# Reordering a decode-attention pipeline: earlier and deeper K/V loads, and an output projection with the weights held still

## The chip, the cores and the metric

The kernel runs on one core of one Trainium2 chip. The metric is the device time of one execution in microseconds, read several times. The span in a profile is about 1.8 us shorter than the time of the same run. "The Trainium skill" is a set of notes on the chip; where the text leans on one of its pages, it names the page.

The engines go by their names in the profile: PE multiplies matrices (its stationary operand, the "weights", is loaded first and the other streams past it), DVE is the vector engine, ACT the scalar engine, POOL is GpSimd, and SyncE (SP) issues the loads. PSUM is the memory that the matmuls add into. The granted clock is PE's clock in the records, as a share of full speed. A hole is a stretch in which the DMA engines are not full; the tail is the time from the last landing of a load to the end.

## The reference

Two independent decode-attention problems, A and B, each for 4 sequences with one new token. There are 32 query heads, 8 K/V heads (4 query heads share one), a window of the last 2048 cache rows and head size 128.

```python
W = min(4096, max(256, Sk // 4))                 # 2048
q = (x @ wq).reshape(B, 1, 32, 128)              # x [4,1,512], wq [512,4096]
k = k_cache[:, :, Sk - W:, :]                    # [4, 8, 2048, 128], likewise v
p = softmax(q k^T * 128**-0.5)
o = p v
y = o.reshape(B, 1, 4096) @ wo                   # wo [4096,512]
return concatenate([y_A, y_B], axis=-1)          # [4,1,1024], bfloat16
```

One (sequence, K/V head) pair is called a chunk: 0.5 MB of K and 0.5 MB of V. There are 64 chunks. With the weights (4 MB of wq and 4 MB of wo for each problem) the kernel reads 84 MB and does little arithmetic on it.

## The kernel before

Chunks run in groups of eight: two K/V heads ("halves") of four sequences. For each chunk K is loaded, DVE transposes it, and four matmuls add its scores to one PSUM bank that holds the whole group. After the eighth chunk come row maximum, exponential, a transpose of the probabilities and the row sums. Then each chunk's V is multiplied (16 small matmuls, "PV"), DVE normalises, and the output projection runs. All loads are issued by SyncE, in program order, so a wait in that list holds back everything behind it:

```python
NK, NKB, NV, BT_LEAD = 4, 4, 4, 2     # raw K, transposed K, V buffers; transposes ahead
PV_OFF = GC + 1                       # GC = 8; PV runs 9 steps after the scores
KV = PV_OFF + 1                       # K loads run 10 steps ahead of V loads

def issue_k(c):
    if c >= NK:
        sp.wait_ge(s_bt, c - NK + 1)      # transposes of K done
    sp.dma_start(kraw[:, c % NK, :], k_src(c)).then_inc(...)
def issue_v(c):
    if c >= NV:
        sp.wait_ge(s_pv, c - NV + 1)      # PV done
    sp.dma_start(vraw[:, c % NV, :], v_src(c)).then_inc(...)

issue_k(0); ...x loads, wq pieces of problem A...
for c in range(1, min(KV, NTOT)):
    issue_k(c)                            # ...and pieces of wo
for s in range(NTOT):
    if s + KV < NTOT:
        issue_k(s + KV)
    issue_v(s)
    ...                                   # pieces of wo and of problem B's wq
```

The projection streams 512 columns of weights past a stationary of 4 columns. The weights are loaded with one head dimension per partition, so every row in DRAM is 512 bfloat16 numbers, 1 KB:

```python
def wo_src(P):
    return probs[P][4].rearrange("(h d) c -> d h c", d=128)
...
for h in range(rep):                                     # do_oproj, per half
    pe.matmul(pob[0:Bsz, 0:D], oT_sb[:, P, hg, :], wo_sb[:, P, hg, :], ...)
```

## Time and profile before

| | before |
|---|---|
| time, median of 3 runs | 230.9 us |
| span of the profiled run | 230.0 us |
| busy: PE / DVE | 146.4 / 102.4 us |
| moved by DMA | 84.16 MB, mean 366 GB/s |

The profiled run (231.78 us) was labelled "slow" in the records. It lies inside the range of later runs of this kernel labelled fast (up to 232.88 us), and a variant of this kernel profiled in a fast run (b1_earlyv below) has nearly the same loss at the end, so I use its structure, not differences of a tenth.

These are the two DMA rows of the page's 40 slices (5.75 us each): busy share of the 16 DMA engines in tenths, and GB/s.

```profile
DMA  6998889999999999999999999999999999999640
GB/s 192 420 416 303 251 269 407 401 399 413 415 415 406 417 392 391 409 396 394 403 392 351 411 393 407 388 402 392 409 385 397 410 395 393 407 392 353 268 180 1
```

There are two holes: slices 4 to 6 (303, 251, 269) and the last four. The windows view puts numbers on them. Its columns are the stretch in us, its length, busy us and instruction count of PE, weight loads, DVE, ACT and POOL, then the granted clock, the DMA share and GB/s.

```profile
0.00:6.00 6.00, 0.00 (x0) 0.00 (x0) 1.25 (x1) 1.28 (x1) 4.83 (x18) 1.00 0.68 198
6.00:20.00 14.00, 3.75 (x131) 3.70 (x132) 1.93 (x3) 0.00 (x0) 5.31 (x1) 1.00 1.01 414
20.00:34.00 14.00, 10.13 (x38) 3.80 (x36) 10.13 (x10) 0.60 (x1) 6.32 (x24) 0.96 0.83 248
34.00:210.00 176.00, 121.06 (x1331) 61.03 (x1338) 86.30 (x105) 7.31 (x17) 11.14 (x40) 0.70 1.03 399
210.00:224.00 14.00, 7.94 (x140) 4.95 (x138) 2.04 (x5) 0.08 (x1) 0.00 (x0) 0.50 0.67 249
224.00:230.00 6.00, 3.54 (x8) 0.86 (x8) 0.74 (x2) 0.00 (x0) 0.00 (x0) 0.71 0.00 1
```

Between 34 and 210 us the DMA engines are full at 399 GB/s. The kernel is bound by bytes plus what the two holes and the start and tail lose. The last part of the chain that ended last shows the tail (start, duration, what):

```profile
215.40 1.39 PE ps L303 x48
216.80 6.36 DMA vraw<-in_B_v_cache_dram
...
223.21 0.60 PE ps L303 x16
223.83 0.24 DVE oT_sb L448
...
224.11 3.56 PE ps L338 x8
227.69 0.68 DVE fin_sb L452
```

The last V load lands at 223.2 us. PV, normalising, a 3.56 us projection (PE near half clock: 0.50 to 0.55 granted from 224 to 227.7 us), a 0.68 us copy and the store follow: 6.8 us after the last landing. What the load queue itself waited for (us in total, times, longest us):

```profile
SPq L183 <- PE ps L303: 94.2, 48, 7.6
SPq L178 <- DVE kb L406: 47.2, 28, 11.6
```

L183 is the issue of V, L178 that of K. The queue waits 94.2 us for PV in all, mostly while loads already issued keep the DMA engines full.

### The profile page before, as it was taken

To read this page: it belongs to the slowest core of one execution; us is meant where nothing else is said; L and a number is where in the kernel's file an instruction comes from. 1 tells how busy PE (TensorE), PEld (TensorE's weight loads), DVE (VectorE), ACT (ScalarE), POOL (GpSimd) and SP (SyncE) were. 2 spreads that over 40 slices of the span, in tenths; PEclk is the share of its full clock that TensorE was granted. 3 is DMA by queue.
4 is the path that set the end of the run, shared out by engine and by line. 5 is a ranking of instruction groups with operands and counts; after the bars stand their busy time and mean duration, and the time that the engine had idled before them with its cause. 6 is when DMAs were issued, how large, how long until landed. Compare 5 with 4: busy or idle time off the path is not lost.

```text
span 230.0 us, 3877 instructions
## 1 busy us (share of the span) xinstructions
PE 146.4 (64%) x1640; PEld 74.3 (32%) x1648; DVE 102.4 (45%) x124; ACT 9.3 (4%) x19; POOL 27.6 (12%) x82
## 2 busy tenths in 40 slices
PE   0026949744499643996789537973698449856735
PEld 0024314311243212465344304441344124424421
DVE  2006767442454243762566335842564447344001
ACT  2001001000100001000010001000100010001000
POOL 7903611110000000000711100120000000000000
PEclk9999985955558755595879955895579656995557
DMA  6998889999999999999999999999999999999640
GB/s 192 420 416 303 251 269 407 401 399 413 415 415 406 417 392 391 409 396 394 403 392 351 411 393 407 388 402 392 409 385 397 410 395 393 407 392 353 268 180 1
DMA packets 29121, 84.16 MB, mean 366 GB/s; under 512 B 3496, under 2 KB 11696, under 8 KB 28080
## 3 DMA queue, kind: packets, MB, share of 16 engines
q1 hardware_dynamic: 29104, 83.91, 95.7%
q8 instruction: 13, 0.21, 0.4%
q14 instruction: 4, 0.03, 0.0%
HBM read 83.89 MB, written 0.01 MB: 365 GB/s over the span
## 4 chain that ended last, share of the span: by engine, by line
DMA 54%; PE 28%; DVE 10%; SPq 3%; issue 2%; ACT 1%; POOL 0%; DVEq 0%; POOLq 0%
DMA kraw<-in_A_k_cache_dram 22%; DMA kraw<-in_B_k_cache_dram 21%; PE ps L283 10%; PE ps L338 7%; DMA vraw<-in_B_v_cache_dram 6%; DVE kb L406 6%; PE ps L303 6%; DMA wq_sb<-in_A_wq_dram 5%; DVE mrow L411 2%; PE ps L318 2%; PE ps L253 2%; PE ps L314 1%; SPq L183 1%; DVE mr L417 1%; SPq L171 1%
## 5 line engine op out<-in xcount | busy, mean ns | idle before, releaser
L406 DVE STREAM_TRANSPOSE kb<-kraw 128x1024 f32<-128x1024 f32 x64 | 78.7, 1236 | 83.9 <-DMA kraw<-in_A_k_cache_dram 41.7
L283 PE MATMUL ps<-kb,lt 128*128 128x512 bf16 x256 | 85.1, 470 | 1.2 <-POOL lt L244 1.2
L303 PE MATMUL ps<-ptu,vraw 128*128 128x4 bf16 x1024 | 36.1, 166 | 27.5 <-DMA vraw<-in_B_v_cache_dram 12.7
L303 PEld LDWEIGHTS ps<-ptu,vraw 128*128 128x128 bf16 x1024 | 34.6, 101 | 46.3 <-DMA vraw<-in_A_v_cache_dram 16.6
L283 PEld LDWEIGHTS ps<-kb,lt 128*128 128x128 bf16 x256 | 23.6, 108 | 31.2 <-issue 18.9
L244 POOL TENSOR_TENSOR lt<-q_sb,msk 128x64 bf16<-128x64 bf16 x64 | 17.5, 292 | 129.2 <-ACT q_sb L373 64.7
L338 PE MATMUL ps<-wo_sb,oT_sb 128*4 128x512 bf16 x64 | 21.1, 489 | 0.5 <-DVE oT_sb L448 0.5
L314 PE MATMUL ps<-identf,mrow 128*1 128x128 f32 x8 | 2.9, 360 | 28.9 <-DVE mrow L411 28.9
L253 PE MATMUL ps<-x_sb,wq_sb 128*128 128x4 bf16 x256 | 7.1, 166 | 17.0 <-DMA wq_sb<-in_A_wq_dram 15.7
L253 PEld LDWEIGHTS ps<-x_sb,wq_sb 128*128 128x128 bf16 x256 | 6.9, 101 | 17.1 <-issue 17.1
L314 PEld LDWEIGHTS ps<-identf,mrow 128*1 128x1 f32 x8 | 0.6, 79 | 35.0 <-DVE mrow L411 35.0
L338 PEld LDWEIGHTS ps<-wo_sb,oT_sb 128*4 128x4 bf16 x64 | 5.7, 99 | 11.0 <-issue 7.1
L430 DVE STREAM_TRANSPOSE ptu<-pu 128x512 bf16<-128x512 bf16 x8 | 5.7, 711 | 6.0 <-ACT pu L385 5.3
L381 ACT ACTIVATE mc<-ps 32x1 f32<-32x1 f32 x8 | 1.3, 161 | 158.3 <-PE ps L316 158.3
L230 POOL MEMSET lt<- 128x8192 bf16 x1 | 6.9, 6926 | 0.0
L448 DVE TENSOR_TENSOR oT_sb<-ps,rinv 128x32 bf16<-128x32 f32 x8 | 1.6, 196 | 11.2 <-PE ps L303 11.2
L411 DVE TENSOR_REDUCE mrow<-ps 128x1 f32<-128x512 f32 x8 | 5.3, 656 | 1.5 <-PE ps L283 1.5
L385 ACT ACTIVATE pu<-ps,nb 128x512 bf16<-128x512 f32 x8 | 5.5, 688 | 6.7 <-DVE nb L422 6.7
L318 PE MATMUL ps<-mc,repf 32*128 32x1 f32 x16 | 4.4, 344 | 2.0 <-ACT mc L381 2.0
L436 DVE TENSOR_REDUCE lsum<-ps 128x32 f32<-128x512 f32 x8 | 5.3, 658 | 0.6 <-remote 0.6
L422 DVE TENSOR_SCALAR nb<-ps 128x1 f32<-128x1 f32 x8 | 1.3, 159 | 8.6 <-PE ps L318 8.6
L318 PEld LDWEIGHTS ps<-mc,repf 32*128 32x128 f32 x16 | 3.8, 290 | 2.7 <-ACT mc L381 2.7
(25 smaller groups left out, 18.7 us busy)
## 6 DMA issues: line engine op xcount, KB each, us to landing
kraw<-in_A_k_cache_dram SPq DMA_DIRECT2D x32, 512.0 KB, 10.7
vraw<-in_A_v_cache_dram SPq DMA_DIRECT2D x32, 512.0 KB, 9.1
kraw<-in_B_k_cache_dram SPq DMA_DIRECT2D x32, 512.0 KB, 9.3
vraw<-in_B_v_cache_dram SPq DMA_DIRECT2D x32, 512.0 KB, 7.5
wq_sb<-in_A_wq_dram SPq DMA_DIRECT2D x4, 1024.0 KB, 8.8
wo_sb<-in_A_wo_dram SPq DMA_DIRECT2D x8, 512.0 KB, 9.5
wq_sb<-in_B_wq_dram SPq DMA_DIRECT2D x4, 1024.0 KB, 13.3
wo_sb<-in_B_wo_dram SPq DMA_DIRECT2D x8, 512.0 KB, 8.3
```

The costliest lines, as they stand in the source:

```text
L230: chain(pool.memset(lt[:, :, :, :, :], 0.0))
L244: pool.tensor_tensor(o_ap, q_ap, m_ap, ALU.mult).then_inc(s_lt, 1)
L253: mm = pe.matmul(qbank[:, h * Bsz:(h + 1) * Bsz], wq_sb[:, P, kt, h * 128:(h + 1) * 128], x_sb[:, P, :, kt], start=(kt == 0), stop=(kt == ...
L283: mm = pe.matmul(sbank[par][:, 0:NS], lt[:, par, c8, je, :], rhs, start=(c8 == 0 and je == 0), stop=(c8 == GC - 1 and je == 3), skip_group ...
L303: mm = pe.matmul(obank[par][:, r0:r0 + rep], vraw[:, c % NV, t * 128:(t + 1) * 128], ptv[:, t, r0:r0 + rep], start=(t == 0), stop=(t == NT ...
L314: pe.transpose(stb[0:1, 0:128], mrow[:, par:par + 1], identf[:, :]).then_inc(s_t1, 1)
L318: pe.matmul(stb[:, 132:133], repf[:, :], mc[:, par:par + 1], start=True, stop=True).then_inc(s_mf, 1)
L338: mm = pe.matmul(pob[0:Bsz, 0:D], oT_sb[:, P, hg, :], wo_sb[:, P, hg, :], start=(u == 0 and ge == 0 and h == 0), stop=(u == NG - 1 and ge ...
L385: act.activation(pu[:, par, 0:NS], sbank[par][:, 0:NS], ACTF.Exp, bias=nb[:, par:par + 1], scale=scale).then_inc(s_exp, 1)
L406: dve.transpose(kb[:, c % NKB, :].bitcast(F32), kraw[:, c % NK, :].bitcast(F32)).then_inc(s_bt, 1)
L411: dve.tensor_reduce(mrow[:, par:par + 1], sbank[par][:, 0:NS], AXL.X, ALU.max).then_inc(s_rm, 1)
L430: dve.transpose(ptu[:, par, 0:NS], pu[:, par, 0:NS]).then_inc(s_pt, 1)
```

## The change

The intent is to keep the load queue ahead at all times, to fill the softmax chain with other work and to make the projection cheap. The core of the diff, cut and in places put in short:

```diff
-    NK = cfg.get("NK", 4); NKB 4; NV 4; BT_LEAD 2; KV = PV_OFF + 1     (set to these)
+    NK 6; NKB 5; NV 9; BT_LEAD 3; KV 9; LS 1 (scores one step ahead)
-        wq_sb = ... [128, NP, KT, HqDh]
+        wq_sb = ... [128, KT, HqDh]            # one buffer for both problems
-        stb, lbank, qbank in three PSUM banks; obank one bank per group parity
+        stb, lbank, qbank share one bank; obank one bank per parity and half
 ...
+            def k_upto(cmax):
+                while kq[0] <= min(cmax, NTOT - 1):
+                    issue_k(kq[0])
+                    kq[0] += 1
+                    if kq[0] == min(NK, KV):
+                        for cv in range(NVPRE):      # NVPRE = NV = 9
+                            issue_v(cv)
+            k_upto(KV - 1)
             for s in range(NTOT):
-                if s + KV < NTOT:
-                    issue_k(s + KV)
-                issue_v(s)
+                k_upto(s + kv_of(s))
+                if s >= NVPRE:
+                    issue_v(s)
 ...
-        woA_steps = [2, 4, 14, 16, 20, 22, 28, 30]; woB_steps = [36, ..., 56]
+        woA_steps = [1, ..., 8]; woB_steps = [20, ..., 34]
 ...                                     # do_oproj, now per half
-                        pe.matmul(pob[0:Bsz, 0:D], oT_sb[:, P, hg, :], wo_sb[:, P, hg, :], ...)
+                for cb in range(NCB):
+                    for h in range(rep):
+                        pe.matmul(o_ap, wo_sb[:, P, hg, cb * 128:(cb + 1) * 128], oT_sb[:, P, hg, :], ...)
 ...                                     # at the end, once
+            pe.transpose(xbank.bitcast(BF16)[0:RF, 0:128], fin1[:, :], identb[:, :])
 ...                                     # DVE, at the end of each group
                     grp_rowmax(grp)
+                    maybe_bt(s + BT_LEAD)          # K transposes between the chain's steps
                     grp_mr(grp)
+                    maybe_bt(s + BT_LEAD + 1)
                     grp_nb(grp)
+                    maybe_bt(s + BT_LEAD + 2)
                     grp_pt(grp)
```

PE likewise runs scores and PV between the chain's steps. DVE transposes five K chunks before it copies the query projection, where it did two.

## The prediction

> **What bounds the kernel now.** The DMA engines. The windows view splits the 230.0 us span: 0 to 6 us at 198 GB/s, 6 to 20 at 414, 20 to 34 at 248, 34 to 210 at 399 (DMA share 1.03, full), 210 to 224 at 249, 224 to 230 nothing; 84 MB in all. The chain that ended last is 54% DMA. PE is busy 146.4 us, DVE 102.4; neither has to be the limit. The Trainium skill ("DMA: Bandwidth & Descriptors", Specifications) gives a fabric ceiling of 435 GB/s; our best stretch (6 to 20 us) is 95% of it. Its 358 GB/s of HBM per core does not bind here: the trace runs at 399 for 176 us.
>
> So the time is bytes at about 400 GB/s plus two holes and a tail:
> 1. Hole at 20 to 34 us. The load queue waits for K transposes, which wait for the query projection (wq lands at 15.7 us) and the first scores; no V is issued before 28.3 us. Against 405 GB/s it loses 14 x (1 - 248/405) = 5.4 us.
> 2. Hole at 210 to 224 us. With 4 V buffers the last V loads wait for PV matmuls, which wait for the last softmax. Loses 14 x (1 - 249/405) = 5.4 us.
> 3. Tail after the last V lands (223.2 us): PV 0.6, normalise 0.25, output projection 3.56 (512 columns at half clock), copy 0.7, store; 6.8 us together.
>
> **What the change does.** K buffers 4 to 6, transposed K 4 to 5, V buffers 4 to 9, paid for by one shared wq buffer. Nine V loads are issued before any wait, so 11.5 MB is queued at the start; at the end V(c) waits only for PV(c-9). Weights are loaded earlier. Transposes and PV fill the softmax chain. The halves stay in groups of two. The output projection becomes 16 matmuls of 4 columns per half (PV's 16 take 0.5 to 0.6 us; I estimate 0.6 to 1.8 us by clock), plus a PE transpose and an ACT copy (about 0.3 us each, from similar ones). Bytes are unchanged.
>
> **On the critical path.** Hole 1 should close: my count of the queue keeps several us of work ahead of the engines, although the first K after the nine V lands near 35 us. Hole 2 should nearly close: the last V is issued before the last softmax ends. Then the tail is PE-paced: eight PV and three projections, ending about 2 us after the last landing; tail 6 to 7.5 us, no gain. The middle may rise from 399 to 405 or 410 GB/s, as its dips (358 to 380) coincide with full K buffers: 0 to 4 us. PE and DVE savings elsewhere are hidden.
>
> Sum: 230.9 - 10.8 - about 2.5 = 217.6 us.
>
> **Predicted: 217.6 us, 8 in 10 between 213.5 and 222.5.** Faster by over 2% 0.94, within 2% 0.04, slower by over 2% 0.02.
>
> **What would show it.** 20 to 34 us at 400 GB/s or more; the 14 us before the last landing full as well; the last landing near 209 to 212 us; DMA's share of the chain up; last landing to end 6 to 7.5 us.
>
> **What would make it wrong.** (a) The DMA rate falls with a deeper queue or bunched wo pieces (1 KB packets). (b) One scratch bank now serves statistics, row sums and query projection and serialises PE; transposes inside the softmax chain wait for K landings and delay PV, so V loads stall and the middle falls below 395 GB/s. (c) PE at half clock (0.5 in much of the middle) needs about 2.7 us per chunk (scores 1.72, PV 0.6, projection) against DMA's 2.6, and must warm up to keep pace. (d) The tail's serial PE work takes longer than I count: 222 us or more.

## The result, and the profile after

| | before | after |
|---|---|---|
| time, median | 231.11 us (15 runs, 228.12 to 232.46) | 220.64 us (12 runs, 220.09 to 221.22) |
| span of the profiled run | 230.0 us | 218.9 us |
| busy: PE / DVE | 146.4 / 102.4 us | 137.8 / 101.4 us |
| mean DMA rate over the span | 366 GB/s | 385 GB/s |

The ratio of the fast runs is 0.9574 (95% interval 0.9546 to 0.9602).

The DMA rows of the page after (slices of 5.47 us):

```profile
DMA  6999999999999999999999999999999999999970
GB/s 186 418 417 412 409 409 408 378 377 375 375 415 406 417 413 410 412 409 394 391 396 399 396 392 393 396 399 402 406 409 408 408 411 407 410 405 410 387 307 12
```

The first hole is gone, the end is much fuller, and a dip to 375 to 378 has appeared in slices 8 to 11 (38 to 60 us); the kernel before ran at 406 from 36 to 60 us. The windows view of the kernel after, in the same columns as above:

```profile
0.00:6.00 6.00, 0.00 (x0) 0.00 (x0) 1.25 (x1) 1.28 (x1) 4.62 (x20) 1.00 0.69 203
6.00:20.00 14.00, 3.55 (x128) 3.50 (x128) 3.00 (x3) 0.00 (x0) 6.01 (x1) 1.00 1.01 418
20.00:34.00 14.00, 8.28 (x28) 3.13 (x28) 3.54 (x4) 0.60 (x1) 4.06 (x16) 1.00 1.03 408
34.00:200.00 166.00, 112.14 (x1369) 60.69 (x1377) 87.93 (x112) 6.55 (x15) 12.31 (x48) 0.68 1.04 401
200.00:210.00 10.00, 8.47 (x132) 5.20 (x130) 3.55 (x7) 0.85 (x2) 0.00 (x0) 0.84 1.00 394
210.00:219.00 9.00, 5.36 (x177) 5.17 (x178) 2.13 (x7) 0.27 (x1) 0.00 (x0) 0.50 0.28 107
```

The end of the chain, from a second profile of the same kernel (the run r_after below, 218.8 us):

```profile
207.44 6.96 DMA vraw<-in_B_v_cache_dram
...
214.45 0.60 PE ps L423 x16
...
215.07 0.20 DVE oT_sb L641
...
215.32 0.60 PE ps L462 x16
...
215.94 0.20 DVE fin L645
...
216.19 0.30 PE ps L557
...
216.51 0.27 ACT fin L577
```

The last V load is issued at 207.4 us and lands at 214.40. Then PV, normalising, a projection of 0.60, a copy, the transpose, another copy and the store take 4.4 us in place of 6.8. In the first profile of this kernel the chain's end has no load in it. Two of its lines:

```profile
213.63 0.46 PE ps L462 x16
...
214.09 1.29 PE ps L423 x48
```

There the last load lands at 214.55 and PE, which has run without a gap since 210.89, ends the last PV at 215.38. So PE and the last load reach the end almost together, now one and now the other a little later. What the load queue waited for in the kernel after:

```profile
SPq L279 <- DVE kb L598: 49.5, 40, 3.2
SPq L286 <- PE ps L423: 33.8, 30, 4.8
```

L286 issues V: its waits for PV fell from 94.2 to 33.8 us.

**Accounting of the 11.1 us of span**, with the rates of the windows above:

- Start hole: (408 - 248) GB/s x 14 us is 2.24 MB, which at 401 GB/s is 5.6 us.
- End hole: before, 3.49 MB from 210 us to the landing at 223.2 take 13.2 us, 4.5 more than at 401 GB/s. After, 200 to 214.4 us moves 4.90 MB, for which 401 GB/s would need 12.2 us, so 2.2 us are still lost. Gain 2.3 us.
- Middle: 401 instead of 399 GB/s over 166 us is 0.8 us.
- Tail after the last landing: 6.8 - 4.4 = 2.4 us.

The sum is 11.1 us, within the rounding of the rates (the first 20 us would add 0.2). The medians differ by only 10.5 us: the profiled run of the kernel before took 0.7 us more than its median, and which term holds that is not known.

### The profile page after: what moved, and what is told of

The parts are those of the page before. It is cut to its first block, busy times and chain, and to the rows that moved or that the text cites. A ratio compares the mean times of both kernels' runs of the same rounds, so it can differ in the third digit from the quotient of the medians.

```text
span 218.9 us, 4309 instructions
## 1 busy us (share of the span) xinstructions
PE 137.8 (63%) x1833; PEld 77.7 (35%) x1841; DVE 101.4 (46%) x131; ACT 9.5 (4%) x20; POOL 27.0 (12%) x84
## 4 chain that ended last, share of the span: by engine, by line
DMA 78%; PE 9%; DVE 5%; SPq 4%; issue 2%; ACT 0%; DVEq 0%
DMA kraw<-in_A_k_cache_dram 40%; DMA kraw<-in_B_k_cache_dram 37%; PE ps L403 4%; DVE kb L598 4%; PE ps L423 3%; SPq L279 2%; PE ps L462 1%; SPq L270 1%; DVE ptu L622 1%; SPq L272 0%; SPq L290 0%; DVE mrow L603 0%; SPq L286 0%; ACT pu L575 0%; DVE oT_sb L641 0%
## 5 line engine op out<-in xcount | busy, mean ns | idle before, releaser
L403 PE MATMUL ps<-kb,lt 128*128 128x512 bf16 x256 | 94.2, 510 | 13.2 <-DVE kb L598 11.9
L423 PEld LDWEIGHTS ps<-ptu,vraw 128*128 128x128 bf16 x1024 | 35.9, 102 | 16.3 <-issue 12.2
L403 PEld LDWEIGHTS ps<-kb,lt 128*128 128x128 bf16 x256 | 25.5, 115 | 45.1 <-issue 24.5
L364 POOL TENSOR_TENSOR lt<-q_sb,msk 128x64 bf16<-128x64 bf16 x64 | 16.4, 293 | 137.5 <-PE ps L403 72.3
L448 PEld LDWEIGHTS ps<-ptu,ones 128*128 128x128 bf16 x8 | 0.8, 104 | 29.4 <-DVE ptu L622 29.4
L462 PE MATMUL ps<-oT_sb,wo_sb 128*128 128x4 bf16 x256 | 9.0, 167 | 1.8 <-DVE oT_sb L641 1.8
L462 PEld LDWEIGHTS ps<-oT_sb,wo_sb 128*128 128x128 bf16 x256 | 7.9, 101 | 2.2 <-DVE oT_sb L641 2.2
L535 PE MATMUL ps<-identf,mr 1*32 1x1 f32 x8 | 1.4, 179 | 7.3 <-DVE mr L609 7.3
L529 PEld LDWEIGHTS ps<-identf,mrow 128*1 128x1 f32 x8 | 0.7, 90 | 13.2 <-DVE mrow L603 12.9
L535 PEld LDWEIGHTS ps<-identf,mr 1*32 1x32 f32 x8 | 0.8, 95 | 12.4 <-DVE mr L609 12.4
L641 DVE TENSOR_TENSOR oT_sb<-ps,rinv 128x16 bf16<-128x16 f32 x16 | 2.7, 170 | 4.3 <-PE ps L423 4.3
```

The lines of the kernel that those rows point to most:

```text
L364: pool.tensor_tensor(o_ap, q_ap, m_ap, ALU.mult).then_inc(s_lt, 1)
L403: mm = pe.matmul(sbank[par][:, 0:NS], lt[:, par, c8, je, :], rhs, start=(c == gstart[grp] and je == 0), stop=(c == gend[grp] and je == 3), ...
L423: mm = pe.matmul(obank[par][ge][:, b * rep:(b + 1) * rep], vbuf(c)[:, t * 128:(t + 1) * 128], ptv[:, t, r0:r0 + rep], start=(t == 0), stop ...
L462: mm = pe.matmul(o_ap, wo_sb[:, P, hg, cb * 128:(cb + 1) * 128], oT_sb[:, P, hg, :], start=(first and cb == 0 and h == 0), stop=(last and ...
```

## The experiments

The theory: the time is bytes at the DMA rate, plus the holes, plus the tail; the change wins by closing the holes (buffer depth and queue order) and by the short projection; the dips in the middle are the 1 KB rows of wo. Rivals: PE and DVE restructuring did it and buffers are incidental; the dips come from engine traffic, the shared bank or waiting V loads. The changed kernel was timed twice (220.64 and 220.53 us median), so I compare experiments with 220.6. They ran on three chips, and only on one of these (that of r_after, e5, e6 and e7) is a run of the changed kernel; the kernel before had medians of 230.86 to 232.02 us on the three, so I read no difference of under 1 us across chips. Line numbers shift by a few between variants.

### e1_wo4k: the same weights in 4 KB rows

```diff
-            return probs[P][4].rearrange("(h d) c -> d h c", d=128)
+            return probs[P][4].rearrange("(j p x) c -> p j x c", p=128, x=4)
```

The bytes are the same but four neighbouring rows go to one partition. Its output is wrong, which doesn't matter for the time.

> The changed kernel with the output-projection weights loaded as 4 KB rows instead of 1 KB rows (same bytes; the result is wrong on purpose). Theory A (the small packets cost DMA rate): 36 to 60 us rises from 379 to about 408 GB/s, 100 to 152 us from 395 to about 408, and the time falls by about 3.5 to 4 us, to 216.5 to 217.5. Rival (the slow stretches come from engine traffic, the shared scratch bank or V loads that wait): the stretches stay below 400 GB/s and the time stays at 220 to 221.

Measured: 217.25 us (217.12 to 217.6, 4 runs), 3.4 us less. Two windows of the changed kernel (the last number is GB/s):

```profile
36.00:60.00 24.00, 17.58 (x160) 8.49 (x161) 16.06 (x18) 0.85 (x2) 4.04 (x16) 0.79 1.06 379
...
100.00:152.00 52.00, 38.38 (x524) 21.77 (x526) 24.48 (x34) 2.30 (x5) 6.15 (x24) 0.63 1.04 395
```

The same two windows of e1_wo4k:

```profile
36.00:60.00 24.00, 17.24 (x161) 8.30 (x161) 16.92 (x19) 0.85 (x2) 4.11 (x16) 0.82 1.03 409
...
100.00:152.00 52.00, 40.47 (x557) 22.54 (x554) 26.24 (x35) 2.29 (x5) 6.16 (x24) 0.63 1.03 409
```

Both stretches in which wo is loaded rise to 409. Theory A holds: in the changed kernel the dips are the rows' size. The rates agree: 30 GB/s over 24 us and 14 over 52 us are 1.45 MB, or 3.5 us at 409. Sixteen pieces cost 3.4 us, 0.21 us each; 0.52 MB at 409 GB/s is 1.28 us, so by this estimate a wo piece takes about 1.5 us and runs at about 350 GB/s. The kernel before loads the same rows, spread over more time, and presumably paid the same; it was not run with longer rows.

### e2_nv4: four V buffers in the new order

```diff
-"NK": 6, "NV": 9,
+"NK": 6, "NV": 4,
```

> The changed kernel with 4 V buffers instead of 9 (the first 4 still issued at once). Theory (the end hole is the V depth): the last 12 us before the last landing fall well below 300 GB/s, the start stays full, time 225 to 227 us, so 4 to 6 us of the 10.5 us gain go. Rival (the gain came from the cheaper projection and the interleaved softmax chain, buffers incidental): 220.5 to 222 us.

Measured: 267.16 us (266.61 to 268.16, 4 runs). Both expectations missed: it is far slower than even the kernel before, which also has four. The queue waits for PV most of the time (us in total, times, longest us):

```profile
SPq L286 <- PE ps L423: 156.0, 52, 11.2
```

From 34 to 250 us the rate is 292 to 335 GB/s in each window that I read. In the new order scores run one step ahead, and more at a group's end, while K is only nine steps ahead of V in the list, so a queue stuck at V starves the scores (this explanation is argued from the order, not shown). The nine V buffers are a condition of the new order, and this run does not isolate the end.

### e9_latev: only the last eight V loads wait as before

```diff
-                    sp.wait_ge(s_pv, vprev[c] + 1)
+                    sp.wait_ge(s_pv, c - 3 if c >= 56 else vprev[c] + 1)
```

> The changed kernel in which only the last eight V loads (chunks 56 to 63) wait as with 4 V buffers, for the PV four chunks back; all else unchanged. Theory (the end hole is the V depth, and only it): the rates to 196 us stay as in the changed kernel, the last 15 us before the last landing fall to 200 to 300 GB/s, time 225 to 228 us. Rival (with the new order PE is early enough that V depth no longer matters at the end): 220.3 to 221.5 us.

Measured: 226.09 us (225.92 to 227.29, 4 runs), 5.5 us more. The rate row of its page:

```profile
GB/s 174 423 418 407 411 410 402 377 376 376 384 417 410 411 412 415 408 403 394 395 392 392 397 398 396 396 394 406 410 407 410 410 407 409 407 361 126 294 357 12
```

Everything up to slice 35 is as in the changed kernel; then 361, 126, 294, 357. The end hole is back. That it costs what the prediction had put on the hole of the kernel before (5.4 us) is chance: this hole is deeper (126 in one slice, where the kernel before falls to 268 and 180 at its end). So V depth at the end is worth about 5 us in the new order.

### e3_nvpre0 and e10_nk4_nvpre0: what closes the start hole

```diff
-"NK": 6, "NV": 9,
+"NK": 6, "NVPRE": 0, "NV": 9,          # e3: no burst of V loads
+"NK": 4, "NVPRE": 0, "NV": 9,          # e10: nor the two extra K buffers
```

> The changed kernel with 9 V buffers but without the early burst: V(s) is issued in step s after K(s+9). Theory (the burst of nine V loads closes the start hole): 20 to 34 us falls to about 250 to 330 GB/s and the time is 223.5 to 226 us. Rival (the deeper K side, 6 raw and 5 transposed buffers, five transposes ahead, closes it): 20 to 34 us stays above 390 and the time stays at 220 to 221.5.

> The changed kernel with neither the early burst of V loads nor the deeper raw K buffers (4 instead of 6); the run without the burst alone kept the start full. Theory (either of the two keeps the in-order load queue from waiting on scores before the first V): with both gone 20 to 34 us falls to 250 to 340 GB/s and the time rises by 3 to 8 us, to 224 to 229. Rival (the five transposes ahead of the query copy are enough alone): 20 to 34 us stays above 390 GB/s; the time may still rise if the middle needs six K buffers, which its rate would show.

Measured: e3 220.57 us (220.43 to 220.78, 4 runs), no change; e10 225.01 us (224.33 to 225.78, 4 runs), 4.4 more. The window of the start hole in e3:

```profile
20.00:34.00 14.00, 10.54 (x40) 4.27 (x40) 8.83 (x10) 0.60 (x1) 4.72 (x19) 1.00 1.03 401
```

The same window in e10:

```profile
20.00:34.00 14.00, 10.03 (x40) 4.15 (x40) 9.12 (x9) 0.60 (x1) 4.57 (x19) 1.00 0.81 280
```

My theory that only the burst of V loads closes the hole fell with e3: without it the start stays at 401 GB/s. In e10 the hole opens again at 280, and 14 x (1 - 280/408) = 4.4 us is the whole loss in time. The middle of e10 is unharmed (408 from 60 to 100 us, 407 from 152 to 196). So six K buffers suffice without the burst; with four and no burst they don't. The list shows the mechanism: with six, the first V issue stands behind the transpose of K chunk 3 and goes out at 21.0 us; with four it stands behind that of chunk 5, which needs the first scores, and goes out at 28.2 us (28.3 in the kernel before). Whether the burst alone would do with four K buffers was not run.

### b1_earlyv: the burst alone, in the kernel before

```diff
                 issue_k(c)
+                if c == NK - 1:
+                    for cv in range(NV):
+                        issue_v(cv)
 ...
-                issue_v(s)
+                if s >= NV:
+                    issue_v(s)
```

> The kernel before with one thing changed: its four V loads are issued right after the fourth K load instead of behind the waits. Theory (the start hole is a queue-order matter: work that waits for nothing stands behind work that waits): 20 to 34 us rises from 248 to 350 GB/s or more, the time falls by 2.5 to 5 us, to 226 to 228.5. Rival (the hole is the latency of the first scores and moves later): 34 to 50 us falls below 350 GB/s and the time falls by under 1.5 us.

Measured: 231.12 us (230.48 to 231.81, 4 runs) against 230.86 for the kernel before on that chip (11 runs, two of them slow and left out of the ratio); ratio 1.0014 (0.996 to 1.0067). No gain. Two windows of it:

```profile
20.00:34.00 14.00, 10.33 (x36) 3.33 (x34) 8.63 (x8) 0.60 (x1) 6.32 (x24) 1.00 0.99 356
34.00:50.00 16.00, 12.21 (x113) 5.98 (x113) 9.58 (x13) 0.85 (x2) 2.06 (x7) 0.78 0.91 323
```

The first hole fills to 356 GB/s, but 34 to 50 us, which the kernel before ran at 401, falls to 323. The rival wins: with four V buffers the queue soon stands at the fifth V, which goes out at 41.5 us, and the hole only moves. Its last slices (360, 261, 173) are as bad as in the kernel before, so part of what is won early is waited for later. Queue order without buffers is worth nothing here.

### e4_oldproj: the projection as it was

```diff
-                for cb in range(NCB): ... 16 matmuls, weights stationary, 4 columns
+                for h in range(rep):
+                    pe.matmul(pob[0:Bsz, 0:D], oT_sb[:, P, hg, :], wo_sb[:, P, hg, :], ...)
 ...            # two copies and two stores; no final transpose
```

> The changed kernel with the earlier form of the output projection (4 matmuls of 512 columns per half, two 4-row stores, no final transpose). Theory (only the tail feels it): last landing unchanged near 212.5 us, three projections in the tail at 1.7 us each at half clock instead of 0.5 to 0.6, minus the transpose and copies: tail 8.5 to 9.5 us instead of 6.3, time 222.5 to 224. Rival (the projection's PE time also delays V loads in the middle): middle falls below 398 GB/s and time over 225. Second rival (prediction: no gain from it): 220 to 221.

Measured: 224.88 us (224.0 to 225.29, 4 runs), 4.3 us more, a little above the expected range. The middle is as before (380, 411, 395, 409 GB/s in the four windows from 36 to 200 us). In the timeline (start, duration, engine, what) the end is paced by PE:

```profile
210.91 1.87 PE L462 MATMUL ps<-wo_sb,oT_sb 128*4 128x512 bf16 x4
...
212.71 1.87 PE L424 MATMUL ps<-ptu,vraw 128*128 128x4 bf16 x64
...
214.50 1.87 PE L462 MATMUL ps<-wo_sb,oT_sb 128*4 128x512 bf16 x4
...
216.30 1.44 PE L424 MATMUL ps<-ptu,vraw 128*128 128x4 bf16 x48
...
218.03 1.87 PE L462 MATMUL ps<-wo_sb,oT_sb 128*4 128x512 bf16 x4 [0.29 <-DVE oT_sb L636]
...
219.93 0.68 DVE L640 CAST fin_sb<-ps 4x512 bf16<-4x512 f32 x1 [1.96 <-PE ps L462]
```

The projections delay PV after PV, and the last one ends near 219.9 us. The last load lands at 214.31 us (214.55 in the changed kernel), and the DMA share from 212 to 214 us is 0.29, near the changed kernel's 0.32, so the loads end alike. The projection is thus worth 4.3 us in the new order, and all of it is at the end: this is the work that stands between the last softmax and the store.

### r_after, e5_nobt, e6_chainfirst: the K transposes inside the softmax chain

r_after is the yardstick on the chip of the next three runs.

> The changed kernel again, as the yardstick on this chip: 220.1 to 221.2 us.

```diff
-"PV_RATE": 1, "LS": 1}
+"PV_RATE": 1, "LS": 1, "BT_IN_CHAIN": 0}      # e5: one K transpose in the chain, not three
```

```diff
                     grp_rowmax(grp)                # e6: none
-                    maybe_bt(s + BT_LEAD)
                     grp_mr(grp)
-                    maybe_bt(s + BT_LEAD + 1)
                     grp_nb(grp)
-                    maybe_bt(s + BT_LEAD + 2)
                     grp_pt(grp)
+                    maybe_bt(s + BT_LEAD)
```

> The changed kernel with only one K transpose inside the softmax chain instead of three. In the trace the last chain but one idles PE for 3.5 us because DVE waits for K landings between the chain's steps; the last scores end 4.4 us after the last K has landed. Theory (those waits delay the tail): the last scores end about 1 to 2 us earlier, last landing unchanged near 212.5, time 219 to 220. Rival (PE at half clock is the tail's limit, the waits are hidden): within 0.3 us of the yardstick.

> The changed kernel with the softmax chain first and no K transpose inside it. Theory (waits for K inside the chain delay PE): PE idles under 2 us at each chain, last scores end 2 us earlier than the yardstick's, tail after the last landing 4.5 us, time 218.5 to 219.5. Rival 1 (hidden): within 0.3 us. Rival 2 (the transposes then come late, the K buffers fill and the DMA starves): middle below 400 GB/s and time over 221.

Measured: r_after 220.53 us (220.5 to 220.96, 4 runs), e5 220.45 (220.39 to 220.67, 5 runs), e6 220.52 (220.36 to 220.82, 4 runs). Nothing. In e6 the chain's end holds the same load:

```profile
207.42 7.03 DMA vraw<-in_B_v_cache_dram
```

It lands at 214.45, as in r_after at 214.40 and in e5 at 214.55, and in e6 PE then waited 0.42 us for it. In e5 the last V load goes out 0.46 us earlier than in r_after (206.98 against 207.44) and lands no earlier: loads already queued, not its issue, set the landing. The chain's waits for K are real but hidden, so the rival that calls them hidden holds in both runs. In these three profiles PE waits 0.42 to 0.66 us for the last V; in the first profile of the changed kernel and in e3 it does not wait. So my prediction's picture of a tail paced by PE holds in some profiles and not in others, by half a microsecond either way.

### e7_xlate: the x loads behind the query weights

```diff
-            for P in range(NP): ...x loads...
             for j in range(NWQ):
                 issue_piece(("wq", 0, j))
+            for P in range(NP): ...x loads...
```

> The changed kernel with the two x loads (8-byte rows) issued after the four query-weight loads instead of before. Theory (they take 1 us of issue time and of the DMA while it should ramp up: 196 and 246 GB/s at 3 to 5 us): 3 to 5 us rises to 400 GB/s and the time falls by 0.5 to 1 us. Rival (the start is latency of the first loads): no change within 0.3 us.

Measured: 219.96 us (219.73 to 220.05, 4 runs) against 220.53, 0.57 us less. Two windows of r_after:

```profile
0.00:6.00 6.00, 0.00 (x0) 0.00 (x0) 1.25 (x1) 1.28 (x1) 4.62 (x20) 1.00 0.72 195
6.00:20.00 14.00, 3.55 (x128) 3.49 (x128) 3.03 (x3) 0.00 (x0) 6.01 (x1) 1.00 1.01 415
```

The same windows of e7:

```profile
0.00:6.00 6.00, 0.00 (x0) 0.00 (x0) 1.25 (x1) 1.28 (x1) 4.62 (x20) 1.00 0.70 258
6.00:20.00 14.00, 3.55 (x128) 3.50 (x128) 3.81 (x4) 0.00 (x0) 5.99 (x1) 1.00 1.03 402
```

From 3 to 5 us the rate is now 410 to 414 GB/s and the first 6 us rise from 195 to 258, but 6 to 20 us falls from 415 to 402, where the 8-byte rows now travel. The direction was right; the gain is near the low end of what was expected because part of it is paid back.

### e11_wosel: a version that beats both

e1 shows that 3.4 us lie in the row size. The 4 KB rows can be made right. With them partition p of a piece holds head p // 32 and rows 4 (p % 32) + x. Sixteen matmuls per half with 0/1 selection matrices and one small copy bring the normalised output into that order. The last half keeps the 1 KB rows, so that the tail gets no extra step; x is loaded as in e7.

```diff
+                for x in range(4):
+                    for hl in range(rep):
+                        pe.matmul(obank[par][pos][:, 64 + 4 * x:64 + 4 * x + 4],
+                                  sel[:, hl, x, :], oT_sb[:, P, g * rep + hl, :],
+                                  start=(hl == 0), stop=(hl == rep - 1))
 ...
+                dve.tensor_copy(oS_sb half, obank[grp % 2][pos][:, 64:80])
 ...            # then the projection as in the changed kernel, with oS_sb
```

> A version meant to beat both, with a right result: output weights of 15 of the 16 halves loaded as 4 KB rows, their mixed row order matched by 16 selection matmuls and one copy per half; x loads after the query weights. Theory: wo's 1 KB rows cost 3.3 us in all, 15/16 of it is won, and the x order 0.55: 36 to 60 and 100 to 152 us at 408 or more, time 216.8 to 217.8 us. Rival (the added matmuls and copies delay the tail or the V loads): 218 to 220.5 us, with the last landing near 211 us and a tail over 5.5.

Measured: 217.33 us (217.04 to 218.04, 6 runs), correct, ratio to the kernel before 0.9419 (0.9381 to 0.9456); 3.3 us below the changed kernel. Three of its windows:

```profile
36.00:60.00 24.00, 17.72 (x161) 8.42 (x161) 17.05 (x21) 0.85 (x2) 4.11 (x16) 0.81 1.03 409
...
100.00:152.00 52.00, 38.96 (x573) 22.62 (x572) 25.41 (x37) 2.29 (x5) 6.16 (x24) 0.70 1.03 407
...
210.00:212.00 2.00, 2.00 (x81) 2.00 (x78) 0.17 (x1) 0.00 (x0) 0.00 (x0) 0.50 0.00 0
```

The middle is at 409 and 407 GB/s and the loads are over by 210 us, but the span is 215.8 us. Now the tail is PE work: no load appears at the end of its chain. Here the order of e6 might pay; that was not run.

## Why the prediction was right or wrong

The time was right: 217.6 us predicted, 220.64 measured, inside 213.5 to 222.5, and faster as forecast. The mechanism, bytes plus holes, was right; three of its terms were not. Point by point:

- **"Hole 1 should close", 5.4 us.** Right in size: 408 GB/s from 20 to 34 us, 5.6 us by the accounting, and opening it again (e10) costs 4.4 us. The prediction counted on the early burst of V loads; e3 shows that the deeper K side does it without the burst, so the reason given was not the one needed.
- **"Hole 2 should nearly close", 5.4 us.** The mechanism is right: e9 opens a hole there again. The size was off: the gain was 2.3 us. About 0.8 of the 5.4 us was counted twice, the stretch from the landing at 223.2 to 224 us, which the tail holds too. And I counted the loss against a rate kept to the last landing. In fact the last loads thin out: in the half microseconds from 212 to 214 us the DMA share of the changed kernel is 0.53, 0.32, 0.24 and 0.20, so 2.2 us are still lost. After the last issue no wait for PV is left to blame: in r_after every load is issued by 207.8 us, the rate is still 397 to 422 GB/s from 207 to 210, and the stretch from 207.8 to the landing (271 GB/s over 6.6 us) alone loses 2.1 us against 401. In the kernel before the stretch after the last issue (216.8 to 223.2 us, 249 GB/s) loses 2.4. So, by this estimate, the waits for PV cost only about 2 us of the hole, and those the depth did win.
- **"The middle may rise from 399 to 405 or 410", about 2.5 us.** Wrong: 401, 0.8 us. I read the dips of the kernel before as full K buffers. e1 shows that in the changed kernel they are the 1 KB rows of wo, 3.4 us in all, which no buffer cures. The prediction names them, under (a), as something that could get worse; it did not see that they were part of the price already (for the kernel before this is presumed).
- **"The last landing near 209 to 212 us."** Wrong: 214.40 us in r_after. It follows from the last two points.
- **"The tail is PE-paced ...; tail 6 to 7.5 us, no gain."** Wrong in size: 4.4 us, a gain of 2.4. PE's part was close. The prediction let eight PV and three projections run on for about 2 us after the landing; the last projection ends 1.7 us after it in the first profile, where PE is the later, and 1.5 us after it in r_after, where the load is. The mis-sized term is what follows: 6 to 7.5 less 2 leaves 4 to 5.5 us for two copies, the transpose and the store, which took 2.6 and 2.9 us. The last projection itself fell from 3.56 to 0.60 us, the low end of the estimate of 0.6 to 1.8. With the old projection in place (e4) PE paces the tail by far, and the kernel is 4.3 us slower.
- **Risks (b) and (c)**, the shared bank and PE at half clock, did not show: the stretches without wo run at 409 to 411 GB/s. Mean granted clock is 0.73 in both kernels.
- **The skill's figures.** "DMA: Bandwidth & Descriptors" (Specifications) gives a fabric ceiling of 435 GB/s; the best long stretch here is 418 (6 to 20 us, after), which agrees. The HBM share of 358 GB/s in the same table does not bind a core alone: 401 over 166 us. "HBM Reference" (Specifications) says as much: a core streaming alone measures well above its share.

The errors partly cancelled: too much was booked for the end hole and the middle (7.9 us for 3.1), too little for the tail (0 for 2.4). That the number landed as near as it did is in part luck.

What stays open: why the end thins out after the last issue (DMA engines that finish unevenly would explain it, but these traces do not tell the engines apart); and whether the burst of V loads ever pays. PE's part of the restructuring (scores one step ahead, scores and PV inside the softmax chain) and the earlier weight loads were never undone alone, nor were the deeper buffers tried in the old order, so their own shares are not shown.

## What to carry to other kernels

When loads bind a kernel, write the time as bytes over rate, plus each hole, plus the tail, and judge each part of a change by the hole that it closes; a load moved forward without a buffer behind it (b1) only moves the hole. Price the rate by row size before reading a dip as a stall: one run with longer rows and a wrong result settles it. Work off the critical path for 200 us, like the projection, can be worth 4 us where it stands between the last load and the store.

## What the Trainium skill lacked or had wrong

- "DMA: Bandwidth & Descriptors" (Specifications) gives 512 bytes and up as the smallest transfer for line rate. Here loads with 1 KB rows run below 4 KB rows: 379 against 409 GB/s in a stretch with about eight such loads, about 350 GB/s for such a load by the estimate in e1. The page's section "Why small descriptors are slow (HBM only)" explains a fixed cost per packet with a 256-byte example; it gives no rate for 1 KB rows (another page times a single descriptor of that size, but no load made of them).
- The same page ("Where 436 GB/s comes from") says that for loads from HBM the 358 GB/s side binds. With one core running, 401 GB/s was held for 166 us and 411 for 40 us, so that sentence needs "with both cores streaming", as "HBM Reference" has it (the page's own note under its measured rates has it too).
- No page that I read has a figure for how the rate fades at the end of a load stream: here the DMA share falls from 1.03 (210 to 211 us) to 0.71, then 0.53, 0.32, 0.24 and 0.20 before the last load's landing (214.55 us in this profile), which costs about 2 us of a bandwidth-bound kernel.
